# Row tiles kept for two sets of vectors, one doubling of k on ScalarE, and two sums of W2 at other steps, in an attention and ResMLP kernel

## The chip, the cores and the metric

One core of a Trainium2 chip runs the whole program. The metric is the device time of one execution in microseconds (us), lower being better. Three runs of the kernel before gave 727.48, 728.22 and 733.85 us, so the median is 728.22 us. The execution that the profiler recorded took 726.85 us; the span from its first to its last instruction was 725.1 us, so that 1.75 us lie around the span.

## The reference

Grouped-query attention over 8 batches (16 query heads, 4 key heads, 384 positions, head size 64), whose output is the input of a residual MLP of width 1024 with a token-mixing and a channel-mixing part:

```python
scores = scale * np.matmul(q, k.transpose(0, 1, 3, 2))
attn = softmax(scores)
x = np.matmul(attn, v)                     # then to (batch, seq, 1024)
a1 = alpha1 * x + beta1
tok = np.einsum('ts,bsd->btd', w_tok, a1)
u = x + lam * tok
a2 = alpha2 * u + beta2
ch = np.maximum(a2 @ w_ch1, 0.0) @ w_ch2   # 1024 -> 4096 -> 1024
out = u + lam * ch
```

## The kernel before

The batches are worked off in four pairs. The MLP of a pair is one product of 2x2 blocks, done with seven block products and sums of blocks in place of eight (the scheme of Strassen and Winograd): the blocks of the weights and of the activations are added and subtracted by VectorE (DVE), and TensorE (PE) multiplies them. A pair has two phases. Phase 0 is the first product (width 1024 to 4096, L704 for pair 0 and L857 later), phase 1 the second one (L777 for pair 0, L923 later). Between the matmuls of phase 1 stand the attention and token mixing of the two batches of the next pair: `scores` (L271), the exponential on ScalarE (ACT, L280), `av` (L306, with L311, L317, L326 and L327 on VectorE behind it), `tok` (L338, with L345 and L351 on VectorE) and `turn` (L415).

**What sets the order.** Nothing is reordered by a scheduler: each engine runs its instructions in the order in which the program issues them, and waits for semaphores. The products are generators that yield after some matmuls; each yield is a step. A table `plan` says what is issued ahead of step `at` of phase `phase` of pair `ps`; `put(ps, phase, at, ...)` appends to it, and entries of one step run in the order in which they were put. `pair(0)` (called the lead) begins at about 59 us in the profile; its phase 1 begins at about 126 us and ends at about 229 us.

**The first product of pair 0** goes over eight groups of hidden units in the order 6, 7, 5, 4, 0, 1, 2, 3. For each, TensorE accumulates in a bank X (products 1, 6, 5, 3, in this order), a bank Y (7, then 4) and, for five of the groups, a bank Z (2). ScalarE copies each intermediate state of X out to SBUF (L712), turns a bias (L719), and applies ReLU (L720, L742, L674). VectorE reads Y twice: L721 after product 7, which must come before product 4 is added to the same bank, and L725 after product 4. L588 and L584 are the sums of the weights of the next group, L744 and L746 the last ReLU and sum of a group.

**Row vectors.** Four vectors of 1024 numbers are needed on all 128 partitions (`vecs`). For alpha1, a product with TensorE does it. For the others, half a vector at a time goes into a row tile (128x512, fp32): the tile is cleared, a DMA on the SP queue writes the half into partitions 0, 32, 64 and 96 (L1059), and a stream shuffle on VectorE copies these four partitions over their quadrants (`to_all`, L1063). alpha2 uses two tiles in `obuf`. lam (index 3) and beta1 (index 1) use tiles of the pool tag "es", which also holds the exponentials: `rows4_on` takes two new tiles for each, and GpSimd (POOL) clears them (L1113). `scale_beta` (L1066) then multiplies half of beta1 by lam.

**k of batch 2.** k is loaded once and doubled within the tile `k2` (`double_k`, L148), after which SP issues a DMA transpose of it (`flip_k`, L174) and four of q (`flip_q`, L178). The q tile has one buffer, so the first load of q of batch 3 on POOL's queue waits until all four transposes of batch 2 have landed. Behind it on that queue stand the load of the third part of the W2 block "11" (L511, into `arena`), which the second product reads, and later loads.

**W2.** The seven block sums of W2 that later pairs use are formed in phase 1 of pair 0 with VectorE (`sum_w2`, L519, 128x2048 each) and stored by SP (L514). `last_w2(c)`, c = 0 to 3, forms the last one ("again"), stores it and frees the slot of its other operand. The products number 4 of the second product, which end it, read "again".

POOL issues the loads that cast from fp32 to bf16, and the stores that add into the output (L459), on DMA queue q0; SP issues transposes, row loads, spills and stores of W2 on q1.

Of the kernel before, what the change touches and what calls it, by code (L numbers as in the profile page):

```python
# [13 lines left out]
def kernel(  # L14
# [21 lines left out]
    nc = tc.nc  # L36
    f32 = mybir.dt.float32
# [12 lines left out]
    P = 128  # L50
# [9 lines left out]
    EB = 4  # L60
# [4 lines left out]
    sb = ST(tc.tile_pool(name="sb", bufs=2))  # L65
# [73 lines left out]
    ks, k2s, qrs = {}, {}, {}  # L139
# [5 lines left out]
        k2s[b] = sb.tile([P, Hkv, 2, NST, D], bf, tag="k2", name="k2", bufs=1)  # L145

    def double_k(b):
        nc.gpsimd.tensor_copy(out=k2s[b][:, :, 1], in_=k2s[b][:, :, 0])  # L148

    def load_k(h):  # L150
        ks[h // 2] = t = hTf[:, 7680 + 384 * h:8448 + 384 * h].bitcast(f32).rearrange(
# [333 lines left out]
    def home(c):  # L485
        return arena[:, HOME + c * 2048:HOME + (c + 1) * 2048]
# [486 lines left out]
    with tc.manual_schedule(engines=order):  # L973
# [22 lines left out]
        rows4 = [obuf[:, i * 512:(i + 1) * 512] for i in range(2)]  # L996
# [60 lines left out]
        def load_row_set(i, half, place):  # L1057
            ap = (moe_alpha1, moe_beta1, moe_alpha2, moe_lam)[i]
            nc.sync.dma_start(out=rows4[place][0:P:32],  # L1059
                              in_=bass.AP(tensor=ap.tensor, offset=ap.offset + half * 512, ap=[[0, 4], [1, 512]]))  # L1060
# [36 lines left out]
        def put(ps, phase, at, *m):  # L1097
            plan.setdefault((ps, phase, at), []).append(m)

        def put_all(ps, phase, table, at=lambda u: u):  # L1100
            for u, ms in table.items():
                for m in ms:
                    put(ps, phase, at(u), *m)

        def put_flips(ps, phase, b, places):
            for u, m in zip(places, ((flip_k, b), *((flip_q, b, i, 2) for i in range(0, NP, 2)))):
                put(ps, phase, u, *m)

        def rows4_on(*sets):
            del rows4[:]  # L1110
            for i, a in enumerate(sets):
                rows4.append(sb.tile([P, 512], f32, tag="es", name="rows4", bufs=EB))
                nc.gpsimd.memset(rows4[i], 0.0)  # L1113
                load_row_set(*a, i)

        put(0, 0, 8, rows4_on, (3, 0), (3, 1))
        put(0, 0, 30, to_all, 3, 0, 0)
        put(0, 0, 34, to_all, 3, 1, 1)
        put(0, 0, 40, rows4_on, (1, 0), (1, 1))
        for i in range(2):  # L1120
            put(0, 0, 54 + 10 * i, to_all, 1, i, i)
            put(0, 0, 59 + 10 * i, scale_beta, i)
        for c in range(4):
            put(0, 0, (50, 72, 74, 44)[c], load_w2, "11", c)
            put(0, 0, (6, 14, 42, 46)[c], cast_w2, "21", c)
            put(0, 1, (41, 43, 45, 47)[c], keep_w2, 1, c)
            put(0, 1, (9, 10, 13, 15)[c], sum_w2, 5, c)
            if c in (1, 2):
                put(0, 1, (3, 25)[c - 1], load_w2, "22", c)
            put(0, 1, (20, 21, 25, 26)[c], sums_first_hid, 2, c)  # L1130
            put(0, 1, (28, 30, 31, 34)[c], sums_first_hid, 4, c)
            put(0, 1, (37, 40, 41, 43)[c], sum_w2, 6, c)
            put(0, 1, (44, 45, 49, 50)[c], sums_first_hid, 3, c)
            put(0, 1, (51, 54, 57, 58)[c], sum_w2, 7, c)
            put(0, 1, (61, 64, 68, 71)[c], last_w2, c)
        put(0, 1, 71, load_w1, order1[3], home(0))
        for u, o in ((77, 5), (79, 7), (81, 6)):
            put(0, 1, u, sum_w1, 0, o)
        for ps in range(NB - 1):
            c = 2 * ps + 2  # L1140
            for i in range(9 if ps else 8):
                put(ps, 0, (4, 12, 16, 20, 24, 54, 58, 62)[i] if ps == 0 else 4 + 7 * i, load_next, c, 1)
                put(ps, 0, 70 + 3 * i if ps == 0 else 91 + 2 * i, load_next, c + 1, 1)
            if ps == 0:
                put(0, 0, 40, double_k, 2)
                put(0, 1, 7, double_k, 3)
            put_flips(ps, 0, c, (44, 46, 50, 54, 58) if ps == 0 else range(76, 86, 2))
            put_all(ps, 1, side(c))
            for u, f, h in zip((8, 14, 14, 27, 32, 33) if ps == 0 else (10, 17, 18, 28, 33, 33),
                               (flip_q, flip_k, flip_q, flip_q, flip_k, flip_q), (0, 0, 2, 4, 2, 6)):  # L1150
                put(ps, 1, u, f, c + 1, h, 2)
            put_all(ps, 1, side(c + 1), lambda u: u + 38)
            for j, u in ((0, 77), (2, 80), (3, 83)) if ps == 0 else ((0, 76), (2, 79), (3, 81)):
                put(ps, 1, u, sums_a, j, 1 if j else 2)

        def steps(ps):
            done = [0, 0]
            for second in pair(ps):
                for f, *a in plan.pop((ps, second, done[second]), []):
                    f(*a)  # L1160
                done[second] += 1
                yield
            for key in [k for k in plan if k[0] == ps]:
                for f, *a in plan.pop(key):
                    f(*a)
# [78 lines left out]
```

## Time and profile before

| | busy us in the span | instructions |
|---|---|---|
| DVE | 554.5 (76%) | 1037 |
| ACT | 373.5 (52%) | 566 |
| POOL | 191.0 (26%) | 242 |

The profiled execution took 726.85 us, its span is 725.1 us, and the granted TensorE clock was 1.0 over it. "Busy" is time in which the engine worked on an instruction; register, semaphore and DMA-issuing instructions are not in it, although a GpSimd instruction that issues a DMA appears on POOL with the time that it took. In the timeline, a row has its start in us from the span's start, its length in us, the engine, the line, the operation, what it writes and reads, the shape and how many instructions were merged; a bracket at its end is how long the engine stood idle before it, and what ended that. An instruction's length can overlap the next one's, since both are pipelined: the step from start to start is what one costs the engine. The chain of waits is the path that ended last, followed back from the last instruction.

Rows that matter for what follows, from the timeline between 60 and 130 us and between 205 and 230 us:

| instruction | where | us |
|---|---|---|
| POOL clears a row tile (L1113), 128x512 fp32 | 67.24 and 74.46, two each | 0.55 each |
| POOL doubles k of batch 2 (L148), 128x768 bf16 | 75.40 | 0.97 |
| VectorE's shuffle (L1063), 128x512 fp32 | 82.27, 83.49, 97.93, 103.78 | 0.72 |
| VectorE's product for beta1 (L1066), 128x512 fp32 | 101.84, 108.04 | 0.68 |
| VectorE's last sums of W2 (L519), 128x2048 bf16 | 213.33, 216.73 | 1.22 |
| ScalarE's ReLU (L742, L674), 128x768 bf16 | all of the first product | 0.84 |

### The profile page before, as it was taken

To read this page: it belongs to the slowest core of one execution; us is meant where nothing else is said; L and a number is where in the kernel's file an instruction comes from. 1 tells how busy PE (TensorE), PEld (TensorE's weight loads), DVE (VectorE), ACT (ScalarE), POOL (GpSimd) and SP (SyncE) were. 2 spreads that over 40 slices of the span, in tenths; PEclk is the share of its full clock that TensorE was granted. 3 is DMA by queue.
4 is the path that set the end of the run, shared out by engine and by line. 5 is a ranking of instruction groups with operands and counts; after the bars stand their busy time and mean duration, and the time that the engine had idled before them with its cause. 6 is when DMAs were issued, how large, how long until landed. Compare 5 with 4: busy or idle time off the path is not lost.

```text
span 725.1 us, 14354 instructions
## 1 busy us (share of the span) xinstructions
PE 711.1 (98%) x5610; PEld 406.3 (56%) x5668; DVE 554.5 (76%) x1037; ACT 373.5 (52%) x566; POOL 191.0 (26%) x242
## 2 busy tenths in 40 slices
PE   8999999999999999999999999999999999999997
PEld 5666555555555666555555566655555566654444
DVE  8888887689899888569678888748867988763344
ACT  7878666545574666634333566653434266650000
POOL 8845324210023341202022344201102223001111
PEclk9999999999999999999999999999999999999999
DMA  9999999999999999969999999989999999947975
GB/s 166 189 238 214 190 185 238 218 221 216 313 281 221 194 159 215 256 187 216 236 228 225 161 173 194 216 215 195 247 256 197 202 123 144 160 132 262 249 228 102
DMA packets 200304, 149.72 MB, mean 206 GB/s; under 512 B 89388, under 2 KB 180884, under 8 KB 199980
## 3 DMA queue, kind: packets, MB, share of 16 engines
q0 software_dynamic: 115152, 70.37, 70.7%
q1 hardware_dynamic: 84396, 77.98, 40.1%
q8 instruction: 44, 0.72, 0.4%
q10 hardware_dynamic: 688, 0.46, 0.2%
q14 instruction: 24, 0.20, 0.1%
HBM read 159.68 MB, written 37.75 MB: 272 GB/s over the span
## 4 chain that ended last, share of the span: by engine, by line
PE 87%; DVE 7%; POOL 2%; issue 2%; ACT 1%; DMA 0%; SPq 0%; ACTq 0%; DVEq 0%; POOLq 0%
PE C L923 28%; PE X L857 17%; PE C L777 9%; PE Y L857 9%; PE sc L271 5%; PE Z L857 4%; PE X L704 4%; PE sc L306 3%; PE sc L338 3%; PE Y L704 2%; PE E L636 1%; PE Z L704 1%; PE tok L338 1%; PE av L306 1%; DVE a1f L326 0%
## 5 line engine op out<-in xcount | busy, mean ns | idle before, releaser
L923 PE MATMUL C<-w,arena 128*128 128x512 bf16 (+2 forms) x711 | 163.7, 372 | 1.6 <-issue 0.3
L280 ACT ACTIVATE es<-sc 128x1024 bf16<-128x1024 f32 x108 | 104.1, 1024 | 115.7 <-PE sc L271 107.4
L923 PEld LDWEIGHTS <-arena 128*128 128x128 bf16 x1040 | 94.7, 98 | 100.5 <-issue 5.1
L459 POOL DMA_DIRECT2D out_dram<-hT x45 | 39.5, 878 | 307.8 <-DVE hT L816 176.7
L862 ACT ACTIVATE hT<-X,bias 128x384 f32<-128x384 f32 x144 | 83.3, 580 | 60.4 <-PE X L857 55.3
L857 PEld LDWEIGHTS <-w 128*128 128x128 bf16 x752 | 73.6, 98 | 48.9
L857 PEld LDWEIGHTS <-pad 128*128 128x128 bf16 x576 | 56.4, 98 | 37.4 <-issue 0.2
L857 PE MATMUL X<-ops,pad 128*128 128x384 bf16 x384 | 70.2, 326 | 0.0
L923 PE MATMUL C<-pad,arena 128*128 128x512 bf16 (+2 forms) x288 | 69.5, 373 | 0.4
L190 POOL DMA_DIRECT2D w<-in_moe_w_ch_dram x47 | 45.6, 1058 | 90.3 <-PE X L857 25.4
L857 PE MATMUL X<-ops,w 128*128 128x384 bf16 x376 | 68.8, 326 | 0.0
L338 PEld LDWEIGHTS <-wtokT 128*128 128x128 bf16 x576 | 37.5, 98 | 16.2 <-issue 3.0
L777 PEld LDWEIGHTS <-arena 128*128 128x128 bf16 x336 | 29.7, 98 | 29.8 <-issue 2.5
L864 DVE TENSOR_TENSOR arena<-Y,hT 128x384 bf16<-128x384 f32 x48 | 26.6, 558 | 20.0 <-ACT hT L862 17.9
L306 PEld LDWEIGHTS <-es 128*128 128x128 bf16 x864 | 32.8, 97 | 11.3
L857 PE MATMUL Z<-ops,w 128*128 128x384 bf16 x192 | 39.0, 326 | 0.0
L271 PE MATMUL sc<-qT,kT 64*128 64x384 bf16 (+2 forms) x504 | 37.2, 271 | 1.7 <-ACT hT L280 0.3
L345 DVE TENSOR_TENSOR xr<-sc,xr 128x384 f32<-128x384 f32 x44 | 24.3, 553 | 17.7 <-PE sc L338 17.7
L280 ACT ACTIVATE hT<-sc 128x1024 bf16<-128x1024 f32 x36 | 35.8, 1031 | 3.7 <-PE sc L271 3.6
L857 PE MATMUL Y<-ops,w 128*128 128x384 bf16 x184 | 37.6, 326 | 0.0
L868 ACT ACTIVATE arena<-X,bias 128x384 bf16<-128x384 f32 x48 | 27.8, 580 | 17.8 <-PE X L857 16.1
L857 PE MATMUL Y<-ops,pad 128*128 128x384 bf16 x192 | 35.1, 326 | 0.0
(207 smaller groups left out, 1177.5 us busy)
## 6 DMA issues: line engine op xcount, KB each, us to landing
w<-in_moe_w_ch_dram POOLq DMA_DIRECT2D x68, 512.0 KB, 10.2
w<-w2s SPq DMA_DIRECT2D x59, 512.0 KB, 5.1
out_dram<-hT POOLq DMA_DIRECT2D x45, 256.0 KB, 6.4
pad<-w2s SPq DMA_DIRECT2D x19, 512.0 KB, 5.0
out_dram<-xr SPq DMA_DIRECT2D x44, 192.0 KB, 7.9
q_raw<-in_q_dram POOLq DMA_DIRECT2D x28, 192.0 KB, 10.1
arena<-in_moe_w_ch_dram POOLq DMA_DIRECT2D x9, 512.0 KB, 15.5
pad<-in_moe_w_ch_dram POOLq DMA_DIRECT2D x9, 512.0 KB, 11.4
```

What stands on the lines that cost most here:

```text
L190: nc.gpsimd.dma_start(out=w1_at[c], in_=w1src[:, :, c * CW * P:(c + 1) * CW * P])
L271: nc.tensor.matmul(out=sc[:, hh, k % 4:k % 4 + n], lhsT=kT_[r, 2 * p // G, BLK[hh][sk], :], rhs=qT_[r, p, st:st + n, :], start=True, stop= ...
L280: nc.scalar.activation(out=e, in_=sc, func=EXP, scale=scale_qk)
L306: nc.tensor.matmul(out=av[:, hh, sq, :], lhsT=ess[k // 4][:, m % 2, k % 4, :], rhs=vb[:, sk, hk, :], start=(sk == 0), stop=(sk == NST - 1))
L338: nc.tensor.matmul(out=ps[:, tt, :], lhsT=wtokT[:, st, tt * P:(tt + 1) * P], rhs=a1s[p][:, st, :], start=(st == 0), stop=(st == NST - 1 an ...
L459: nc.gpsimd.dma_start(out=by_tok(out[b])[:, ms, dw * 512:(dw + 1) * 512], in_=o, accum_op=ADD)
L704: nc.tensor.matmul(out=ps[:, :n], lhsT=tb[G, o][:, dt, e * P:(e + 1) * P], rhs=opb(FIRST1[o], n)[:, dt], start=(o in (1, 2, 7) and dt == 0 ...
L777: nc.tensor.matmul(out=x, lhsT=lead_hid[:, t, FIRST2[o], ms * P:(ms + 1) * P], rhs=rhs[:, t % 4 * 512:(t % 4 + 1) * 512], start=(o in (1, ...
L857: nc.tensor.matmul(out=ps, lhsT=tb[g, o][:, dt, e * P:(e + 1) * P], rhs=opb(LEFT1[o])[:, dt], start=(o in (1, 2, 7) and dt == 0), stop=(dt ...
L862: nc.scalar.activation(out=snap[o, e], in_=ps, func=IDENT, bias=hi if o == 5 else lo)
L868: nc.scalar.activation(out=hid[:, t, 4], in_=ps, func=RELU, bias=hi)
L923: nc.tensor.matmul(out=x, lhsT=hid[:, t, LEFT2[o], ms * P:(ms + 1) * P], rhs=rhs[:, t % 4 * 512 + c0:t % 4 * 512 + c1], start=((not last o ...
```

## The change

`rows4_on` takes two tiles and clears them only on its first call; the second call (beta1) loads into the same two tiles. The list `rows4` keeps the two tiles of `obuf` as its first entries, so the new ones have indices 2 and 3. The second call stands at step 37 in place of 40; the two shuffles of beta1 stand at steps 49 and 63 in place of 54 and 64, each product of `scale_beta` one step behind its shuffle, at 50 and 64 in place of 59 and 69. `double_k(2)` is issued at step 35 in place of 40, to ScalarE in place of GpSimd. `last_w2(2)` stands at step 66 of phase 1 in place of 68; `last_w2(3)` stays at step 71, but is put into the plan last, so it is issued behind the load of W1 and the `av` of head pair 6 of batch 3, which have the same step.

In the order of the engines this comes to the following. POOL loses two memsets and the copy of k. ScalarE gets the copy between the second and third of four copies L712 of group 4. On VectorE, L1063 and L1066 of the first half of beta1 stand together behind the L584 that ran at 92.88 us; L1066 of the second half stands behind the shuffle that ran at 103.78 us; the L519 that ran at 213.33 us stands ahead of the L793 that ran at 210.24 us, and the one that ran at 216.73 us stands behind the L327 that ran at 219.28 us. TensorE's and SP's orders are the same as before. The two row loads of beta1 on SP now wait for the shuffles of lam in place of POOL's memsets, and the transpose of k waits for ScalarE in place of POOL.

```diff
     def double_k(b):
-        nc.gpsimd.tensor_copy(out=k2s[b][:, :, 1], in_=k2s[b][:, :, 0])
+        (nc.scalar.copy if b == 2 else nc.gpsimd.tensor_copy)(out=k2s[b][:, :, 1], in_=k2s[b][:, :, 0])
...
         def rows4_on(*sets):
-            del rows4[:]
+            if len(rows4) == 2:
+                for i in range(2):
+                    rows4.append(sb.tile([P, 512], f32, tag="es", name="rows4", bufs=EB))
+                    nc.gpsimd.memset(rows4[2 + i], 0.0)
             for i, a in enumerate(sets):
-                rows4.append(sb.tile([P, 512], f32, tag="es", name="rows4", bufs=EB))
-                nc.gpsimd.memset(rows4[i], 0.0)
-                load_row_set(*a, i)
+                load_row_set(*a, 2 + i)
 
         put(0, 0, 8, rows4_on, (3, 0), (3, 1))
-        put(0, 0, 30, to_all, 3, 0, 0)
-        put(0, 0, 34, to_all, 3, 1, 1)
-        put(0, 0, 40, rows4_on, (1, 0), (1, 1))
+        put(0, 0, 30, to_all, 3, 0, 2)
+        put(0, 0, 34, to_all, 3, 1, 3)
+        put(0, 0, 37, rows4_on, (1, 0), (1, 1))
         for i in range(2):
-            put(0, 0, 54 + 10 * i, to_all, 1, i, i)
-            put(0, 0, 59 + 10 * i, scale_beta, i)
+            put(0, 0, 49 + 14 * i, to_all, 1, i, 2 + i)
+            put(0, 0, 50 + 14 * i, scale_beta, i)
...
-            put(0, 1, (61, 64, 68, 71)[c], last_w2, c)
+            if c < 3:
+                put(0, 1, (61, 64, 66)[c], last_w2, c)
         put(0, 1, 71, load_w1, order1[3], home(0))
...
             if ps == 0:
-                put(0, 0, 40, double_k, 2)
+                put(0, 0, 35, double_k, 2)
                 put(0, 1, 7, double_k, 3)
...
+        put(0, 1, 71, last_w2, 3)
```

## The prediction

> **What bounds the kernel now.** The page's first part says that TensorE works for almost the whole span, so an edit pays only where TensorE stands still.
>
> ```profile
> PE 711.1 (98%) x5610; PEld 406.3 (56%) x5668; DVE 554.5 (76%) x1037; ACT 373.5 (52%) x566; POOL 191.0 (26%) x242
> ```
>
> All edits lie in pair 0, so I next read TensorE's timeline there, first product and then second one.
>
> ```profile
> 78.69 1.46 PE L704 MATMUL Y<-ops,pad 128*128 128x384 bf16 x8 [0.95 <-DVE arena L721]
> ...
> 99.92 0.81 PE L704 MATMUL Y<-ops,w 128*128 128x384 bf16 x4 [0.16 <-DVE arena L725]
> ...
> 109.30 0.81 PE L704 MATMUL Y<-ops,w 128*128 128x384 bf16 x4
> ```
>
> ```profile
> 219.89 0.68 PE L338 MATMUL sc<-a,wtokT 128*128 128x128 bf16 x9 [0.72 <-DVE a L327]
> ```
>
> The eight X matmuls ahead of the first three rows start at 76.21, 98.29 and 107.73, and eight take 1.31 us in the chain of waits, so TensorE was ready at 77.52, 99.60 and 109.04. Ahead of the last row four matmuls of 512 columns start at 218.14 and take 0.86 in the chain: ready at 219.00. It stands for 1.17, 0.32, 0.26 and 0.89 us, 2.64 in all, and each time VectorE ends the wait. What made VectorE late is in its timeline beside POOL's, and for the last wait in the chain.
>
> ```profile
> 74.44 1.25 DVE L744 TENSOR_SCALAR arena<-arena 128x768 bf16<-128x768 bf16 x1
> 75.79 0.98 DVE L746 TENSOR_TENSOR arena<-arena 128x768 bf16<-128x768 bf16 x1
> ...
> 81.33 0.35 DVE L744 TENSOR_SCALAR arena<-arena 128x768 bf16<-128x768 bf16 x1
> 81.78 0.56 DVE L746 TENSOR_TENSOR arena<-arena 128x768 bf16<-128x768 bf16 x1
> ```
>
> ```profile
> 74.46 1.01 POOL L1113 MEMSET rows<- 128x512 f32 x2
> 75.40 0.97 POOL L148 COPY k<-k 128x768 bf16<-128x768 bf16 x1
> ```
>
> ```profile
> 213.42 1.14 DVE w L519
> ...
> 216.82 1.13 DVE pad L519
> ...
> 219.28 0.57 DVE a L327
> ```
>
> The same two operations take 0.35 and 0.56 us at 81 us, and 1.25 and 0.98 while POOL clears the tiles and copies k: 1.32 us lost.
>
> **The change, part by part.** *POOL's two memsets and the copy go.* L744 becomes 0.90 shorter, L746 0.42. The wait at 78.69 does not shrink by all of that, since L721, which ends it, also needs the bias that ScalarE writes in L719 at 77.51 (0.15 long), and that follows TensorE's own matmuls. L721 started at 78.02 and can start at about 77.70: a gain of 0.32 to 0.35, taken as 0.35; bounds 0 (the slowness had another cause) and 1.17. POOL gains nothing of its own: it next waits until 81.75 for VectorE's L744.
>
> The Trainium skill, SBUF — State Buffer, section "Who interferes with whom", says that GpSimd and a VectorE operation that uses both its ports take a shared pair of ports as a lock: whoever starts first keeps it. L744 stands 20 ns ahead of the memset in the records; by that rule POOL would have waited, L744's 0.90 us would have another cause and stay, and the sum below would be about 1.1 in place of 1.45. Twenty ns are too few to say who came first.
>
> *The copy goes to ScalarE.* The nearest row is ScalarE's ReLU of the same shape, 0.84 us (POOL's copy: 0.97). It is issued behind the copy L712 at 83.44, starts about 83.86 and ends at 84.70; the next L712 started at 84.74 after 0.82 idle. Cost 0. If the copy takes twice that, L712 ends at 86.0 in place of 85.2, and product 3, which needs it at 85.85, waits some 0.2 us; that is the upper bound, and nothing below zero.
>
> *Beta1's rows and shuffles.* The row loads wait for lam's shuffles (the second ends at 84.2, less 0.35) in place of a memset that ended at 75.5. In the old run they were issued at 75.04 and 75.7, and the only 16 packets of q1 between 77.5 and 80 us are theirs, so they land within 5 us: about 89.5. The first shuffle and product now come behind L584 at 92.88, where VectorE idled 1.73 us before 95.30; they cost 0.62 + 0.60 = 1.22 there (start to start at 97.93 and 108.04): hidden, with 0.5 to spare. Without the shuffle at 97.93, L725 comes 0.62 earlier, and the 0.32 at 99.92 is gone; without the product at 108.04, L725 comes 0.60 earlier and the 0.26 at 109.30 is gone. The second product moves from 101.84 to behind the shuffle at 103.78, the work between moving up by as much. If that work is held by its loads, up to 0.24 + 0.60 − 0.60 = 0.24 of it shows. Taken: 0.58 gained; bounds 0.34 and 0.58.
>
> *The sums of W2.* The L519 of 213.33 fits mostly into VectorE's idle 0.75 us ahead of 210.24: it runs 209.42 to 210.56 and pushes L793 by 0.32. The chain from 210.24 to L327 loses two L519 (1.14 and 1.13), but L793 of 216.13 must wait for ScalarE's copy, which ends at 215.59: it starts at 215.63, not at 215.31. So L327 starts at 216.13 → 215.63, less 1.14: 219.28 − 0.50 − 1.14 = 217.64, and the wait of 0.89 is gone. Next late is the following head pair: its L327 started at 221.76, 2.48 behind the first one, and now has the second L519 ahead: 217.64 + 1.14 + 2.48 = 221.26. Its `tok` at 222.37 followed it directly, so 0.50 is what remains. Bounds 0 and 0.89. The late L519 ends at 219.3, and the matmuls that read its result come at 219.5 at the earliest. Behind its store SP has only two spills, which waited until 223.4 and 225.1 for VectorE.
>
> *SP's queue.* The transpose of k started at 76.39, the moment that POOL's copy was done. It now waits for ScalarE and for the second row load ahead of it, both about 84.55: 8.2 us later. Behind it stand the four transposes of q (80.81 to 99.56 with 4.2 us of waits for q, now covered) and two loads (102.71 and 105.98, read from 135.5 on). Scores of batch 2 need the transposes only at 127. But POOL waits for them:
>
> ```profile
> 110.47 0.74 POOL L453 DMA_DIRECT2D q_raw<-in_q_dram  x1 [3.81 <-DMA qT<-q_raw]
> 114.63 0.74 POOL L511 DMA_DIRECT2D arena<-in_moe_w_ch_dram  x1 [3.42 <-DVE bias L716]
> ```
>
> The second row is the part of "11" that the ninth matmul of the second product reads (128.9, or 128.0 after the gains). By SP's issue times, with the waits for q gone, the transposes land 4.2 us later (109.9 becomes 114.1), and the load is issued at 115.4; by the packets, 8.2 us later (118.1), and it is issued at 119.4. In both cases q0 is still full: the load ahead landed at 121.4, and this one took the last 2.6 of its 10.4 us, so it lands near 125. Cost 0.
>
> ```profile
> q0 software_dynamic: 4695, 4.00, 90.2%
> q1 hardware_dynamic: 4694, 1.24, 38.3%
> ```
>
> These are the two queues from 81 to 109.5 us, packets first: one for one, so the transposes cannot hurry while q0 is full; I lean to 118.1. The Trainium skill, DMA: Bandwidth & Descriptors, section "Queues, rings and completion order", has the engines take turns between queues packet by packet; the trace agrees, and the rule speaks for the later time, against this change.
>
> Sum: 0.35 + 0.58 + 0.50 = 1.43 us. The profiled span becomes 723.7, its time 726.85 − 1.43 = 725.4. The median of the runs shown is 1.37 above that execution; two runs stand at 727.48 and 728.22 (mean 727.85), so I expect 726.4.
>
> **The rivals.** *POOL was not to blame, or the gain of that part is missed.* For it: 20 ns; against it: L744 at 67.50 also took 0.97, beside the other two memsets. Then 1.1 us are gained: 726.8. *The gain is given back later.* The chain has, in pair 2, 2.38 us at 371.83 in which a DMA ends last, and DMAs are busy at 90% in nearly every slice; against it, these transfers are issued by waits on TensorE and VectorE, which move with it. Then 727.9. *Slower: the late transposes hold the load of "11".* The load is issued at 119.4 and TensorE needs it at 128.0, so it decides from 8.6 us to landing on. At its own former 10.4 us it lands at 129.8: 1.8 lost, 0.4 slower than before, 728.2. At 17.2, the median of such loads between 60 and 130 us, it lands at 136.6: 8.6 lost, 735.0. For it speaks that the two SP loads now share engines with it; against it, that its own share of queue time was 2.6 us.
>
> **How the numbers follow.** My forecast has 0.60, the first rival 0.15, the second 0.14, the slower one 0.09 (half of it beyond 1%), other 0.02. Low end: all 2.64 us recovered from the profiled 726.85, 724.2. High end: the second rival and the mild slower case at the median of before plus the bounds 0.2 + 0.24 and some 0.5 of scatter between two runs, 729.2. One per cent, 7.3 us, is about what a measurement of this kernel can tell from no change (its three runs spread by 6.4): faster 0.02, same 0.93, slower 0.05.
>
> **What would show it.** L744 and L746 of the third group at 0.35 and 0.56; TensorE's waits on L721, L725 (two) and L327 at 0.8, 0, 0 and below 0.4; the transposes' end and the landing of the load of "11" before 128. It is wrong if a shuffle waits for its row, if L712 behind the copy is late, or if TensorE stands at the ninth matmul of the second product.

## The result, and the profile after

The median of 21 runs is 726.01 us (lowest 725.38) beside 729.63 us (lowest 726.87) for 21 runs of the kernel before on the same chips. The ratio is 0.9953, with a 95% interval of 0.9933 to 0.9974: between 0.26% and 0.67% faster, which is within one per cent. Single executions of either kernel came out up to some 15 us above its fastest, and the profiles of such executions of the changed kernel and its variants lose it outside the change (5 to 8 us at a load ahead of the first product in two, 3 to 4 us at a load near 578 us in two others), so in what follows a part is judged by the lengths of its stage and by TensorE's waits rather than by medians.

Three profiles were taken of the changed kernel. The rows here are of the third, an execution of 726.19 us with a span of 724.4. First part 1 of its page:

```profile
PE 715.1 (99%) x5668; PEld 406.4 (56%) x5668; DVE 551.6 (76%) x1037; ACT 374.9 (52%) x567; POOL 189.1 (26%) x239
```

POOL has three instructions fewer and ScalarE one more. TensorE's 4.0 us more are no more work: some matmul records can be missing from a trace, and this one has 5668 where that of before had 5610. Next TensorE's timeline at the four places of the forecast:

```profile
78.65 1.15 PE L704 MATMUL Y<-ops,pad 128*128 128x384 bf16 x6 [0.63 <-DVE arena L721]
...
99.58 0.81 PE L704 MATMUL Y<-ops,w 128*128 128x384 bf16 x4
...
108.70 0.81 PE L704 MATMUL Y<-ops,w 128*128 128x384 bf16 x4
...
218.30 0.67 PE L338 MATMUL sc<-a,wtokT 128*128 128x128 bf16 x9
...
221.16 0.68 PE L338 MATMUL sc<-a,wtokT 128*128 128x128 bf16 x9 [0.30 <-DVE a L327]
```

The wait at 78.65 is still there, and smaller (bracket 0.95 before, 0.63 now). The two L725 waits are gone: TensorE goes from the eight X matmuls, which start at 98.27 and 107.40, to the next in 1.31 and 1.30 us, as fast as eight take. The wait for L327 has moved on by one head pair and is smaller (0.72 to 0.30). A bracket counts from the end of the matmul ahead, and matmuls overlap by about 0.16; counted from start to start, beyond a normal step, the waits are 0.79, 0, 0 and 0.46 us, against 1.12, 0.32, 0.26 and 0.89 before. (The prediction put the first at 1.17, from a mean of eight matmuls in the chain.)

The stages have these lengths, from the first matmul of one to the first of the next, in us:

| profile | first product of pair 0 | second product of pair 0 | first product of pair 1 |
|---|---|---|---|
| before | 68.36 | 102.93 | 72.97 |
| before, once more | 68.13 | 102.91 | 72.97 |
| changed, second profile | 67.40 | 102.40 | 73.85 |
| changed, third profile | 67.39 | 102.41 | 73.53 |

So the change took 0.96 us out of the first product and 0.52 out of the second, 1.48 in all; the forecast had 0.93 and 0.50. Against the second profile of before it is 0.73 and 0.51, 1.24 in all. The lowest times, 725.38 and 726.87, differ by the same 1.5 us. In the first product of pair 1 up to 0.9 us more can be lost.

### The profile page after: what moved, and what is told of

The parts are those of the page before. It is cut to its first block, busy times and chain, and to the rows that moved or that the text cites. A ratio compares the mean times of both kernels' runs of the same rounds, so it can differ in the third digit from the quotient of the medians.

```text
span 738.9 us, 14402 instructions
## 1 busy us (share of the span) xinstructions
PE 718.5 (97%) x5668; PEld 406.9 (55%) x5668; DVE 554.1 (75%) x1037; ACT 374.7 (51%) x567; POOL 189.3 (26%) x239
## 4 chain that ended last, share of the span: by engine, by line
PE 80%; DMA 11%; DVE 3%; SPq 2%; POOL 2%; issue 1%; ACT 1%; POOLq 0%; DVEq 0%; ACTq 0%
PE C L923 26%; PE X L857 17%; PE C L777 9%; PE Y L857 8%; PE Z L857 4%; DMA out_dram<-xr 4%; PE sc L271 4%; PE sc L306 3%; PE sc L338 3%; PE X L704 2%; DMA w<-w2s 2%; SPq L178 2%; DMA qT<-q_raw 2%; DMA arena<-in_moe_w_ch_dram 2%; DMA arena<-q_raw 1%; PE Y L704 1%
## 5 line engine op out<-in xcount | busy, mean ns | idle before, releaser
L923 PE MATMUL C<-w,arena 128*128 128x512 bf16 (+2 forms) x744 | 172.2, 378 | 5.2 <-DMA w<-w2s 5.2
L864 DVE TENSOR_TENSOR arena<-Y,hT 128x384 bf16<-128x384 f32 x48 | 26.6, 557 | 21.3 <-ACT hT L862 19.4
L777 PE MATMUL C<-w,arena 128*128 128x512 bf16 x144 | 35.5, 379 | 0.0
```

What stands on the lines that cost most here:

```text
L777: nc.tensor.matmul(out=x, lhsT=lead_hid[:, t, FIRST2[o], ms * P:(ms + 1) * P], rhs=rhs[:, t % 4 * 512:(t % 4 + 1) * 512], start=(o in (1, ...
L864: tt(out=hid[:, t, 1], in0=Y[e][:, :S], in1=snap[5, e], op=ADD)
L923: nc.tensor.matmul(out=x, lhsT=hid[:, t, LEFT2[o], ms * P:(ms + 1) * P], rhs=rhs[:, t % 4 * 512 + c0:t % 4 * 512 + c1], start=((not last o ...
```

## The experiments

**The changed kernel and the kernel before, once more.**

> The changed kernel once more, for a profile without the disturbance of the first one. The theory that the four waits of TensorE add up: L744 and L746 of the third group near 0.35 and 0.56 us, TensorE waits about 0.8 us on L721 (before 1.17), not at all on the two L725, at most 0.4 on L327 of the last head pair; the time 1.4 us below the kernel before. The rival of the late load: TensorE waits at the ninth matmul of the second product (about 130 us) for the arena load of block 11, by 1 us or more, as the first profile of the changed kernel shows (2.3 us); then the gain of the other parts has to exceed 1.4 us elsewhere, or the time lies within 1 us of before.

> The changed kernel a third time, since its first two profiles fell on disturbed executions (spans of 738.9 and 733.7 us). Theory: without disturbance the load of block 11 that the ninth matmul of the second product reads lands at about 127 us, as in the profile with the sums put back (127.19), less than 1 us ahead of TensorE, and TensorE does not wait for it; waits on L721 0.8, on L725 none, on the last L327 0.46 us. Rival: the wait for that load is part of the changed kernel and shows here too, by 1 us or more.

> The kernel before, unchanged, profiled once more: TensorE waits 1.12 us on L721, 0.32 and 0.26 on the two L725, 0.89 on L327; stages 68.4 and 102.9 us. Against itself the ratio should hold 1.0. If the slowdown of the load queue near 91 us comes with the later transposes, it isn't here: 1.5 MB on q0 between 88 and 100 us and no wait at the ninth matmul of the second product. If it comes of itself, it can be here too: 1.2 MB or less and a load that lands behind 128 us. One profile without it doesn't tell the two apart.

A ratio is the time beside that of the kernel before, run on the same chip, with its 95% interval in brackets. Measured for the changed kernel: 726.97 and 727.29 us, ratios 0.9964 [0.9926, 1.0002] and 0.9978 [0.9944, 1.0013]; lowest 725.39 and 725.48. The kernel before against itself gave 0.9995 [0.9955, 1.0035]. The waits of the forecast came out alike in all profiles of the changed kernel. Before, once more, waited 0.88 us for L721, not 1.12; since L744 and L746 took 1.01 and 0.98 there in place of 1.25 and 0.98, the wait followed VectorE's 0.24 us one for one.

**The sums of W2 back at their old steps.**

```diff
-            if c < 3:
-                put(0, 1, (61, 64, 66)[c], last_w2, c)
+            put(0, 1, (61, 64, 68, 71)[c], last_w2, c)
...
-        put(0, 1, 71, last_w2, 3)
```

> The changed kernel with the last two sums of W2 at their old steps. If the waits add up, the wait of about 0.9 us on L327 at the end of the second product is back and the kernel loses 0.5 us against the changed one. If the sums did nothing, the wait is there in neither kernel and the times are equal.

727.2 us, ratio 0.9958 [0.9925, 0.9991]; stages 67.41 and 102.98 us. TensorE's timeline has the wait for L327 back on the head pair ahead, and none at the next one:

```profile
219.22 0.68 PE L338 MATMUL sc<-a,wtokT 128*128 128x128 bf16 x9 [0.72 <-DVE a L327]
...
221.71 0.68 PE L338 MATMUL sc<-a,wtokT 128*128 128x128 bf16 x9
```

The second product gave back 0.57 us, the first nothing: the moved sums are worth what the second product gained, and little else is in it.

**The shuffles and products of beta1 back at their old steps.**

```diff
-            put(0, 0, 49 + 14 * i, to_all, 1, i, 2 + i)
-            put(0, 0, 50 + 14 * i, scale_beta, i)
+            put(0, 0, 54 + 10 * i, to_all, 1, i, 2 + i)
+            put(0, 0, 59 + 10 * i, scale_beta, i)
```

> The changed kernel with the shuffles and products of beta1 at their old steps (54, 59, 64, 69); the row tiles are still cleared once. If the shuffles were what made L725 late, TensorE waits again by about 0.3 us twice, ahead of product 7 or 4 of the groups at about 99 and 109 us, and 0.6 us are lost. If ScalarE's bias (L719) bounds these places, the waits are the same as in the changed kernel.

728.11 us, ratio 0.999 [0.9944, 1.0037]; first product 67.96 us. Both waits for L725 are back, with 0.32 and 0.26 us, while L721 stays at 0.79. The first of them in TensorE's timeline:

```profile
100.56 0.81 PE L704 MATMUL Y<-ops,w 128*128 128x384 bf16 x4 [0.16 <-DVE arena L725]
```

**The two parts of POOL's work, one at a time.** The changed kernel with the doubling of k on GpSimd (no memsets, copy on POOL), and the kernel before with it on ScalarE (memsets, no copy on POOL):

```diff
-        (nc.scalar.copy if b == 2 else nc.gpsimd.tensor_copy)(out=k2s[b][:, :, 1], in_=k2s[b][:, :, 0])
+        nc.gpsimd.tensor_copy(out=k2s[b][:, :, 1], in_=k2s[b][:, :, 0])
```

> The changed kernel with the doubling of k of batch 2 on GpSimd again, at the same step 35. The copy then starts at about 74.5 us with no memset ahead. If a GpSimd copy blocks VectorE as the memset seemed to, L744 of the third group takes about 1.25 us again and L746 about 0.56, and 0.35 us of the gain at L721 are lost. If only memsets do it, L744 takes 0.36. The transposes of batch 2 still wait for the second row load of beta1, so the load of block 11 is as late as in the changed kernel; if it is not, ScalarE was what held them.

```diff
-        nc.gpsimd.tensor_copy(out=k2s[b][:, :, 1], in_=k2s[b][:, :, 0])
+        (nc.scalar.copy if b == 2 else nc.gpsimd.tensor_copy)(out=k2s[b][:, :, 1], in_=k2s[b][:, :, 0])
...
-                put(0, 0, 40, double_k, 2)
+                put(0, 0, 35, double_k, 2)
```

> The kernel before with the doubling of k of batch 2 on ScalarE at step 35; the second pair of memsets stays. With a GpSimd copy alone on the same queue L744 of the third group took 0.92 us, and L746 0.56. If the lock goes by who is first, or covers memsets too, L744 takes 1.2 us beside the memsets and L746, now without the copy, 0.56 us in place of 0.98; TensorE's wait on L721 is then between 0.8 and 1.12 us, since 0.42 of VectorE's delay is gone: 0.8. If the memset does not block, L744 takes 0.36.

727.82 us (ratio 0.9975 [0.9932, 1.0017]) and 728.33 us (1.0002 [0.9967, 1.0037]). What POOL ran beside L744, in the first and then in the second:

```profile
74.32 0.84 POOL L148 COPY k<-k 128x768 bf16<-128x768 bf16 x1
```

```profile
74.97 1.00 POOL L1113 MEMSET rows<- 128x512 f32 x2
```

VectorE's timeline of the first and, below it, of the second:

```profile
74.46 0.92 DVE L744 TENSOR_SCALAR arena<-arena 128x768 bf16<-128x768 bf16 x1
75.49 0.56 DVE L746 TENSOR_TENSOR arena<-arena 128x768 bf16<-128x768 bf16 x1
...
77.72 1.28 DVE L721 SCALAR_TENSOR_TENSOR arena<-Y,bias,hT 128x384 bf16<-128x384 f32 x2 [0.34 <-ACT bias L719]
```

```profile
74.69 1.50 DVE L744 TENSOR_SCALAR arena<-arena 128x768 bf16<-128x768 bf16 x1
76.30 0.56 DVE L746 TENSOR_TENSOR arena<-arena 128x768 bf16<-128x768 bf16 x1
```

Either of POOL's operations makes L744 long; L746 is long only where the copy ran beside it. Yet TensorE's wait for L721 was 0.79 with the copy on POOL, as in the changed kernel, for VectorE then still stood 0.34 us idle until ScalarE's bias was there. With the memsets kept it was 0.945, where 0.8 was expected: L744 had become longer. That is 0.175 less than in the first profile of before, just as L744 and L746 together are shorter by 0.17, but 0.065 more than in the second one, where they are longer by 0.07. So taking the memsets away brings the whole gain at this wait, and moving the copy as well adds nothing; what moving the copy alone is worth is not told from the difference between the two profiles of before. Nor does the copy on POOL bring the transposes back to their old place: SP issued that of k at 84.74 us, behind the later row loads.

**ScalarE ahead of L721.** If ScalarE's bias is what is left, the ReLU L674 in front of it must be worth something:

```diff
-                if (o, e) == ((5, 1) if quick else (1, 1)) and i:
+                if (o, e) == (((3, 1) if i == 2 else (5, 1)) if quick else (1, 1)) and i:
```

> The changed kernel, with ScalarE's ReLU of group 7 (L674) issued behind product 3 of group 5 in place of ahead of its biases. If ScalarE bounds what is left of the wait on L721 (0.79 us in every variant so far, whether L744 took 0.36 or 0.92), L719 comes about 0.6 us earlier and the wait falls to 0.2 to 0.4 us; the time gains about 0.5. If VectorE still bounds it, the wait stays at 0.79.

726.07 us, lowest 725.07, ratio 0.9971 [0.9932, 1.0009]; first product 67.02 us. ScalarE's timeline of the changed kernel, and then of this one:

```profile
77.05 0.85 ACT L674 ACTIVATE arena<-arena 128x768 bf16<-128x768 bf16 x1
77.80 0.15 ACT L719 COPY bias<-X 128x1 f32<-128x1 f32 x1
```

```profile
77.15 0.16 ACT L719 COPY bias<-X 128x1 f32<-128x1 f32 x1 [0.20 <-PE X L704]
...
78.53 0.83 ACT L674 ACTIVATE arena<-arena 128x768 bf16<-128x768 bf16 x1
```

The bias comes 0.65 us earlier (0.45 if counted from the first matmul of the product, at 58.26 and 58.06), it now waits for TensorE and not for ScalarE's own work, and TensorE's wait for L721 falls from 0.79 to 0.36.

**The late transposes and the load of "11".** The same kernel was run again, and then with the load of the third part of "11" put ahead of the first q load on POOL's queue:

```diff
-            put(0, 0, (50, 72, 74, 44)[c], load_w2, "11", c)
+            put(0, 0, (50, 72, 73, 44)[c], load_w2, "11", c)
```

> The kernel with ScalarE's late ReLU a second time, beside the kernel before: 1.9 us below it if the waits add up (1.48 us of the changed kernel plus 0.44), and its stages as in its first profile: 67.0 us for the first product and 102.4 for the second of pair 0. If the gain is given back later by loads of W1, the first product of pair 1 takes up to 73.9 us in place of 72.97.

> The kernel with ScalarE's late ReLU, and in addition the load of the third part of block 11 ahead of the first load of q of batch 3 on POOL's queue (step 73 in place of 74). If the queue position is what makes that load late, it is issued when its own slot is free (about 114 us or earlier) and lands 1 us or more ahead of the 123.9 us of the late-ReLU kernel; TensorE does not wait for it in either, so an undisturbed execution takes the same time, 725.1 at the lowest. If the transposes do not matter for it, it lands at 123.9 as before.

729.13 us (ratio 0.9997 [0.9966, 1.0029]) and 730.61 us (0.9975 [0.9928, 1.0023]), with the first product at 67.00 and 66.99, so the gain of the ReLU held there. The median of the first shows none of the 1.9 us that were expected, and in both profiles TensorE stood at the ninth matmul of the second product. POOL's issue and TensorE's wait, first without and then with the load put ahead:

```profile
117.21 0.75 POOL L511 DMA_DIRECT2D arena<-in_moe_w_ch_dram  x1
...
130.21 2.75 PE L777 MATMUL C<-arena 128*128 128x512 bf16 x12 [2.21 <-DMA arena<-in_moe_w_ch_dram]
```

```profile
108.11 0.74 POOL L511 DMA_DIRECT2D arena<-in_moe_w_ch_dram  x1 [2.78 <-DVE arena L725]
...
129.44 2.75 PE L777 MATMUL C<-arena 128*128 128x512 bf16 x12 [1.67 <-DMA arena<-in_moe_w_ch_dram]
```

Issued 9.1 us earlier, the load landed only 0.8 us earlier (129.40 against 130.17), where more than 1 us ahead of 123.9 was expected. So in these two profiles it is not its place behind the q load that makes it late; what queue q0 still had to move ahead of it fits. (The profile with the load put ahead lost more than this: its second product took 109.94 us, with a further wait of 1.61 us for a load near 175 us and one of 2.32 us for L327 near 199.) In both profiles q0 had moved little between 88 and 100 us. Its row of that window in the third profile of the changed kernel, where the load landed at 123.83, and in the profile with the wait of 2.21:

```profile
q0 software_dynamic: 1539, 1.52, 81.9%
```

```profile
q0 software_dynamic: 1120, 1.10, 92.3%
```

(packets, MB, share of 16 engines' time). From 91.6 to 96.1 us both queues together moved mostly 44 to 106 GB/s there, after some 200 ahead, and a packet of q0 took 0.923 × 192 / 1120 = 0.16 us of an engine's time in place of 0.10. The first profile of the changed kernel (an execution of 740.66 us) shows the same, with 1.17 MB and a wait of 2.32 us.

**The transposes moved out of that window.**

```diff
-                put(0, 0, 35, double_k, 2)
+                put(0, 0, 49, double_k, 2)
...
-            put_flips(ps, 0, c, (44, 46, 50, 54, 58) if ps == 0 else range(76, 86, 2))
+            put_flips(ps, 0, c, (50, 50, 52, 54, 58) if ps == 0 else range(76, 86, 2))
```

> The changed kernel with the doubling of k of batch 2 one group later (step 49; the first two transposes at step 50): the transposes of batch 2 begin about 9 us later again, at 94 us. If the late transposes hold the load of block 11, its issue moves from 116 to about 125 us, it lands at 134 to 137 us, and TensorE waits 5 to 9 us at the ninth matmul of the second product: the time is 4 to 8 us above the changed kernel. If the load queue is what bounds its landing, it lands at 127 to 129 and costs at most 1 us.

725.91 us, lowest 725.46, ratio 0.9946 [0.9912, 0.998]. The wait of 5 to 9 us that I expected did not come. SP issued the transpose of k at 93.87 in place of 85.00, but POOL's q load followed at 115.53 in place of 113.30 and the load of "11" landed at 123.55 in place of 123.83: the transposes took 21.7 us in place of 28.3 from SP's first issue to the q load. With 2.10 MB of q0 done in the window in place of 1.52, they met an emptier queue.

Last, both edits together, the ReLU later and the transposes later:

> The changed kernel with both edits: the ReLU of group 5 issued two steps earlier, and the doubling of k at step 49 with the first two transposes at step 50. Theory: TensorE's wait on L721 near 78.7 is 0.36 us in place of 0.79, the first product (L704 to L777) takes 67.0 us and the second (L777 to L857) 102.4 when the ninth matmul doesn't wait. If the transposes of batch 2 are what makes the load queue slow down near 91 us, this kernel, in which they start at about 96 us, moves at least 2 MB on q0 between 88 and 100 us and its ninth matmul never waits; its median lies about 0.4 us below that of the changed kernel, near 725.6. Rival: the slowdown comes of itself; then q0 can move 1.2 MB or less there and the ninth matmul waits 1.8 to 2.4 us, as in three profiles of kernels that had the transposes early.

The expectation has the ReLU "two steps earlier"; the edit is the one above, two steps later. Measured: 726.8 us, lowest 724.95 of all kernels, ratio 0.9955 [0.9918, 0.9992]. In its profile the first product took 67.00 us, the wait for L721 was 0.36, q0 moved 2.29 MB between 88 and 100 us, and the ninth matmul did not wait. The second product took 103.35: two waits of 0.45 and 0.56 us near 205 and 212 us, where VectorE's L317 was late, took its gain away. Such waits, of 0.46 to 0.87 us at one of the two places, are in three other profiles too (spread back, copy on POOL, transposes late), there behind SP's stores of W2. By the medians it is not told from the changed kernel.

## Why the prediction held, point by point

*The time: 726.4 us forecast, 726.01 measured.* That they agree to 0.4 us is luck in part: two more medians of the changed kernel are 726.97 and 727.29, and the medians of the first measurement lie 3.62 us apart, over twice the forecast gain of 1.43. What bears the forecast out are the lowest times, 1.49 us apart, and the stages, with 1.24 to 1.48.

*L721: 0.35 forecast, 0.33 measured against the first profile of before, 0.09 against the second,* whose wait was 0.88 and not 1.12. The mechanism was right in both halves. POOL's work had lengthened L744 and L746 (1.25 and 0.98 before, 0.36 and 0.56 after), and ScalarE's bias capped what TensorE saw of it. The size rests on the execution: where the memsets began 0.20 us ahead of L744 in place of 0.02 behind, L744 had lost 0.24 less. VectorE's timeline of the changed kernel shows that cap:

```profile
74.72 0.36 DVE L744 TENSOR_SCALAR arena<-arena 128x768 bf16<-128x768 bf16 x1
75.19 0.56 DVE L746 TENSOR_TENSOR arena<-arena 128x768 bf16<-128x768 bf16 x1
...
77.98 1.28 DVE L721 SCALAR_TENSOR_TENSOR arena<-Y,bias,hT 128x384 bf16<-128x384 f32 x2 [0.91 <-ACT bias L719]
```

Of 1.32 us that VectorE got back, 0.91 is now idle time before L721. A detail was wrong: the prediction let the bias follow TensorE's matmuls, but L674 stood ahead of it on ScalarE, as the ReLU experiment showed, and 0.43 us more could be had there. The first rival (POOL not to blame) falls with the two experiments on POOL's parts. So does the reading of the Trainium skill, SBUF — State Buffer, section "Who interferes with whom", that L744, 20 ns ahead of the memset, would have kept the shared ports: its 0.90 us did go. The price of 1.1 us that the prediction put on this reading does not follow from its own cap: L746's 0.42 alone would have let L721 start 0.32 us sooner, and the sum would have stayed near 1.4.

*The two L725: 0.58 forecast, 0.58 measured*, and 0.58 again when the shuffles went back. The second product of beta1 found its place without the 0.24 of the lower bound.

*L327: 0.50 forecast, 0.43 measured at the wait.* The next head pair is what is late next, as said, with 0.46 us left in place of 0.39. VectorE's timeline:

```profile
208.71 1.22 DVE L519 TENSOR_TENSOR w<-w,pad 128x2048 bf16<-128x2048 bf16 x1
...
214.92 0.69 DVE L793 TENSOR_TENSOR hT<-C,hT 128x512 f32<-128x512 f32 x1 [0.24 <-ACT hT L790]
...
216.93 0.56 DVE L327 TENSOR_TENSOR a<-a1f,vecs 128x384 bf16<-128x384 f32 x1
217.40 1.22 DVE L519 TENSOR_TENSOR pad<-pad 128x2048 bf16<-128x2048 bf16 x1
...
220.55 0.56 DVE L327 TENSOR_TENSOR a<-a1f,vecs 128x384 bf16<-128x384 f32 x1
```

The second L327 comes 3.62 us after the first, 1.14 + 2.48 as worked out. The remaining 0.1 us of the second product's 0.52 is spread over steps too short to name.

*The copy on ScalarE at no cost: right.* It starts at 83.79, takes 0.84, and the next L712 at 84.72 is not late:

```profile
83.79 0.84 ACT L148 COPY k<-k 128x768 bf16<-128x768 bf16 x1
84.72 0.48 ACT L712 COPY hT<-X 128x384 f32<-128x384 f32 x1
```

*The late transposes at no cost: right in seven of ten profiles, for a partly wrong reason.* SP issued them 8.6 us later (8.2 forecast). POOL's timeline in the third profile:

```profile
113.30 0.74 POOL L453 DMA_DIRECT2D q_raw<-in_q_dram  x1 [10.83 <-DMA qT<-q_raw]
114.03 0.75 POOL L511 DMA_DIRECT2D arena<-in_moe_w_ch_dram  x1
```

The q load went out 2.8 us later than before, less than either of the two figures weighed (4.2 and 8.2); in the other profiles with transposes from about 85 us on it went out between 113.1 and 117.5, 2.6 to 7.0 us later than before (the changed kernel's second profile aside, where the first product began 9 us later than in the others). The sharing of the engines packet by packet is in the rows, but it did not shift the transposes' end by their whole delay. While q1 stood free, q0 went ahead: it moved 2.41 MB from 76 to 88 us against 1.97 before, and so had less left. The landing near 125 was met: 123.8, and up to 127.6 in the other profiles in which TensorE did not wait for it.

*The slower rival* was right about the place and the size of the mild case, 1.8 us forecast and 1.83 to 2.38 measured at the ninth matmul in three profiles, and wrong about the cause: the load's late issue alone does not make the wait. What makes q0 slow near 91 us in those three stays open. They are the three of the ten profiles with transposes from about 85 us on in which q0 moved least from 88 to 100 us (1.09 to 1.17 MB, against 1.28 to 1.52). The wait was in none of the profiles of the kernel before (two) and of the kernels whose transposes were moved out of that window (two), which is too few to lay it on the transposes: a shorter dip to about 100 GB/s stands near 90 us with the late transposes too, when none of them had begun.

*The second rival, the gain given back later,* finds a loss of its size, but not one shown to come of the gain. In pair 1 VectorE's sums waited for a load of W1, and L864 behind them came late to TensorE. VectorE and TensorE in the third profile:

```profile
271.05 0.69 DVE L535 TENSOR_TENSOR pad<-w 128x1024 bf16<-128x1024 bf16 x1 [2.97 <-DMA w<-in_moe_w_ch_dram]
...
272.39 1.01 DVE L864 TENSOR_TENSOR arena<-Y,hT 128x384 bf16<-128x384 f32 x2
```

```profile
272.99 1.46 PE L857 MATMUL Y<-ops,pad 128*128 128x384 bf16 x8 [0.40 <-DVE arena L864]
```

That cost 0.56 us here, 0.88 in the second profile (the stages of 73.53 and 73.85 above) and 0.84 with both edits. In these three L535 started 43.0 to 43.3 us behind the pair's first matmul, in the other profiles, those of before included, 40.0 to 42.3 us behind it, and there the stage has its 72.97. That the pair begins earlier does not decide it: with the ReLU later it began at 227.48, earlier than in any other profile, and did not wait. And the kernel before, once more, has the same wait in pair 2 (a bracket of 0.77 us near 439 us, for L864 behind a load of W1). So the landing of such loads varies from one execution to the next in both kernels; whether a shorter product ahead of them makes the wait more frequent stays open.

## What to carry to other kernels

An engine off the critical path can still cost time by making another one's instruction longer: compare the same instruction's length with and without company before its own work is called free. Then ask what ends the wait next: here 1.32 us saved on VectorE were worth 0.33, since ScalarE's bias was ready only that much sooner than VectorE, and one ReLU issued two steps later was worth 0.43 at the same wait. When a gain of tenths is at stake, read it from stage lengths and waits in several profiles; the medians of the same kernel moved by more.

## What the runs showed of the hardware

L744 beside POOL did not become slower by a factor, it ended a fixed time behind POOL's instruction: 0.22, 0.21, 0.22 and 0.22 us behind the end of the memsets or the copy (before, before once more, copy on ScalarE only, copy on POOL). The L744 one group earlier, beside the first pair of memsets, which every kernel has, ended 0.21 to 0.22 us behind them. It made no difference whether L744 started 280 ns ahead of the memset or 250 ns behind it. POOL's DMA-issuing instruction lengthens it too: with one from 74.39 to 75.13, L744 took 0.54 and ended at 75.29, 0.16 us behind (transposes late). Where L744 stood first, such an instruction still ran (until 74.47 before and 74.98 with the copy on ScalarE only), so POOL may have held what both need without a gap; that was not tried by itself.

Transposes that start 8.6 or 9 us later need not end as much later: twice the time from the first issue to the q load behind them became shorter (34.1, 28.3 and 21.7 us). In both cases the other queue had moved more by then: 2.41 MB in place of 1.97 from 76 to 88 us, and 2.10 in place of 1.52 from 88 to 100.
